# Attention feeding a mixture of experts: where the routing weights are multiplied in, and in which order the first layer's products run

## The chip, the core and the metric

The kernel runs on one core of one Trainium2 chip. That core has five engines with instruction queues of their own, each taken in order: TensorE (PE in the profile: matmuls, with PEld for its weight loads), VectorE (DVE), ScalarE (ACT), GpSimd (POOL) and SyncE (SP, which only issues transfers). They wait for each other through semaphores. The metric is the device time of one execution in microseconds, as the median of several.

## The reference, cut to what matters

The first half is attention over 4 batches, 8 heads, 768 positions and 64 features. Three heads use a full causal mask; five see only 4 first positions and a window of 64. Its result, put back into rows of 512 features, is the input of the second half, in which every token goes through all four experts, weighted by normalised probabilities:

```python
scores = scale * np.matmul(q, k.transpose(0, 1, 3, 2))
scores = np.where(mask[None, :, :, :], scores, -1000000000.0)
a = softmax(scores)                       # cut: written out in the reference
attn_out = np.matmul(a, v)
x = np.ascontiguousarray(attn_out.transpose(0, 2, 1, 3)).reshape(B * S, H * D)   # 3072 x 512

p = domain_probs / (domain_probs.sum(-1, keepdims=True) + 1e-09)
for e in range(E):                        # E = 4 experts, 512 -> 1024 -> 512
    h = np.maximum(x @ w1[e], 0.0)
    out += p[:, e:e + 1] * (h @ w2[e])
```

## The kernel before

Tokens are in 24 tiles of 128. Attention is made in eight groups of 384 positions (three tiles each), numbered 0 to 7. The first four tiles go through the experts in a plain way; the other twenty in ten pairs of tiles (`pair_steps`; here pair 0 to pair 9, tiles 4 and 5 to tiles 22 and 23). Attention of later groups is recorded between the steps of the experts: every step of the experts yields its nominal time and a share, and a plan tells how far each attention group should be once so much weighted time is spent.

Because p is positive, p * relu(x @ w1) is relu((p * x) @ w1). So VectorE multiplies the input of each expert by that expert's probabilities first. This is one instruction of 1024 elements per partition, or two of 512 where a pair straddles two attention groups. The factors, `pB`, are fp32 and come by a transfer into a single buffer.

```python
def scale_inputs(nt0, e):
    ...                                   # cut: xs = scaled(e), the slot of expert e
    for g, c0, t0, n in pieces(nt0):
        require(g)                        # attention group g is recorded to its end first
        ...
        nc.vector.tensor_tensor(          # L1078
            out=o, in0=xin, in1=pb.to_broadcast([P, DMP, n, P]), op=ALU.mult
        )
```

A pair's first layer treats experts 0 and 1 as ordinary products (`plain_layer1`, L1115: eight steps of eight matmuls 128 x 256, each step ended by a ReLU on ScalarE), and experts 3 and 2 (`EW`) by a Winograd scheme with seven half-size products instead of eight. Each product is eight matmuls of 128 columns (L1144). Partial results are kept by ScalarE (`keep`) and added by VectorE (`add`, L1160, followed by a clamp at zero, L1166). Each expert has two banks of PSUM, x and y, which its products share; the second expert takes the same two in reverse, so a product often has to wait until the previous content of its bank has been read:

```python
product(x, w1_part(e, 0, 0), x_part(e, 0, 0), True);  keep(0, x)          # 1
product(z, w1_part(e, 1, 0), x_part(e, 0, 1), True);  add(0, z, 0)        # 2
product(x, t(1), x_sum(1), False);                    keep(1, x)          # 3
product(y, t(0), x_sum(0), True);                     keep(2, y)          # 4
minus(x_part(e, 0, 1), x_part(e, 0, 1), x_sum(1))
product(x, w1_part(e, 0, 1), x_part(e, 1, 0), False); add(2, x, 3)        # 5
product(y, w1_part(e, 1, 1), x_part(e, 0, 1), False); add(1, y, 2)        # 6
product(x, t(2), x_part(e, 1, 1), False)              # 7, then ReLU on ScalarE
# cut: a yield (ns, 0.5) after each product
```

`scaled_sums(e)` makes x_sum(0), x_sum(1) and a difference out of the scaled input (three VectorE instructions; L1092 and L951). The order of the first layer, with a for the products of expert 3, b for those of expert 2 and n01 for plain steps of experts 0 and 1:

```python
for steps, op in (
    ((a, a, n01), lambda: scale_inputs(nt0, EW[1])),
    ((a, a, n01), lambda: scale_inputs(nt0, 1)),
    ((a, n01), lambda: scaled_sums(EW[1])),
    ((a, a, n01), lambda: load_probs(nxt) if nxt is not None else None),
    ((b, b, n01), lambda: first_sum(0)),
    ((b, b, n01), lambda: first_sum(EW[0])),
    ((b, n01), lambda: last_weight_sum(E - 1) if nt0 == pair0 else None),
    ((b, b, n01), None),
):
```

The second layer runs over all four experts at once, also with seven products, of sixteen matmuls with 256 columns each (L1228). In between VectorE makes sums of hidden blocks in place (`second_sum`, `third_sum`, `fourth_sum`, L951), and the two first scalings of the next pair stand near the end:

```python
yield from product(x, A11, b(0, 0), True);  keep(0, x);  second_sum(0); second_sum(1)   # 1
yield from product(y, A12, b(1, 0), True);  add(0, y, 0, 0);  third_sum(0)              # 2
yield from product(x, S2, t(1), False);     keep(1, x);  third_sum(1)                   # 3
yield from product(y, S1, t(0), True);      keep(2, y);  fourth_sum(0); fourth_sum(1)   # 4
yield from product(x, S3, b(0, 1), False);  add(2, x, 1, 1);  scale_inputs(nxt, 0)      # 5
yield from product(y, S4, b(1, 1), False);  add(1, y, 0, 1);  scale_inputs(nxt, EW[0])  # 6
yield from product(x, A22, t(2), False);    scaled_sums(EW[0])                          # 7
# cut: yields, stores of the result, the conditions for the last pair
```

Of the kernel before, what the change touches and what calls it, by code (L numbers as in the profile page):

```python
# [10 lines left out]
FP32 = mybir.dt.float32  # L11
# [7 lines left out]
def kernel(  # L19
# [34 lines left out]
    P = 128  # L54
    B, H, S, D = q.shape
    E, DM, F = moe_w1.shape
# [474 lines left out]
    def mm_ns(cols):  # L531
        return cols / 2.4 + 2.5

    def attention(b, c):
# [282 lines left out]
        if first:  # L817
            yield from transposes(0)
            yield from scores(0)
            sink_row(1)  # L820
            sink_row(3)
            nc.scalar.copy(out=bS[:, 2, :], in_=bS[:, 1, :])
            yield from transposes(1)
            yield from scores(2)
            sink_row(4)
            sink_row(5)
            sink_row(7)
            yield from both(scores(1), values(0))
            yield from transposes(2)
            yield from both(scores(3), values(2))  # L830
            x_transposes(0)
            yield from scores(4)
            yield from transposes(3)
            yield from values(1)
            yield from both(scores(5), values(3))
            yield from both(scores(6), values(4))
            yield from both(scores(7), values(6))
            yield from values(5)
            x_transposes(6)
            yield from values(7)  # L840
            tick(LAG)
            small_things()
        else:
            order = (0, 2, 6, 1, 3, 5, 7, 4) if by_dma else (0, 2, 1, 3, 6, 5, 7, 4)
            more = divmod(g + 1, NCH) if g + 1 < G else None
            if not by_dma:
                sink_rows(b, c)

            def behind_values(h):
                if more and not RETR[h]:  # L850
                    load_v(*more, [h])
            if by_dma:
                keys_to_rows(b, c)
                yield 500.0
            else:
                yield from transposes(0)
                yield from transposes(1)

            waiting = []
            for n, h in enumerate(order):  # L860
                v_steps, done = iter(()), None
                ahead = sum(len(score_tiles(x)) for x in (*waiting, h))
                if len(waiting) > 1 or (waiting and ahead > 6):
                    done = waiting.pop(0)
                    v_steps = values(done)
                yield from both(scores(h), v_steps)
                if done is not None:
                    behind_values(done)
                waiting.append(h)
                if n == 1 and by_dma:  # L870
                    keys_to_windows(b, c)
                    sink_rows(b, c)
                if n == 3 and more and g > 1:
                    transpose_k(*more)

                    load_q(*more)
                if not by_dma and n in (1, 3):
                    yield from transposes({1: 3, 3: 2}[n])
            if more:
                if g == 1:  # L880
                    load_probs(pair0)
                    transpose_k(*more)
                transpose_q(*more)
            for h in waiting:
                yield from values(h)
                behind_values(h)
# [154 lines left out]
    PT = 2  # L1041
# [25 lines left out]
    def scale_inputs(nt0, e):  # L1067

        if xs_of[0] is None:
            xs_of[0] = moe.tile([P, E * DMP * PC], FP16, name="xs", tag="xs", bufs=1)  # L1070
        xs = scaled(e)
        for g, c0, t0, n in pieces(nt0):
            require(g)
            xin = xT[g][:, :, c0 : c0 + n * P].rearrange("p c (t x) -> p c t x", t=n)
            o = xs[:, :, t0 * P : (t0 + n) * P].rearrange("p c (t x) -> p c t x", t=n)
            pb = pB_of[nt0][:, t0 : t0 + n, e, :]
            pb = pb.rearrange("p t (c x) -> p c t x", c=1)
            nc.vector.tensor_tensor(  # L1078
                out=o, in0=xin, in1=pb.to_broadcast([P, DMP, n, P]), op=ALU.mult
            )  # L1080
# [9 lines left out]
    def scaled_sums(e):  # L1090

        nc.vector.tensor_tensor(  # L1092
            out=x_sum(0), in0=x_part(e, 1, 0), in1=x_part(e, 1, 1), op=ALU.add
        )
        minus(x_sum(1), x_sum(0), x_part(e, 0, 0))
        minus(x_part(e, 1, 0), x_part(e, 0, 0), x_part(e, 1, 0))
# [5 lines left out]
        )  # L1102


    PSHARE = 1.57

    def pair_steps(nt0, nxt):

        def plain_layer1(e):
            xs = scaled(e)  # L1110
            for f0 in range(0, FTP, 2):
                ps = bank()
                for f in range(2):
                    for ct in range(DMP):
                        nc.tensor.matmul(  # L1115
                            out=ps[:, f * PC : (f + 1) * PC],
                            lhsT=w1sb[:, e * DMP + ct, (f0 + f) * P : (f0 + f + 1) * P],
                            rhs=xs[:, ct, :],
                            start=(ct == 0),
                            stop=(ct == DMP - 1),  # L1120
                        )
                b0 = 2 * (f0 // HT)
                k0 = e * HT + f0 % HT
                nc.scalar.activation(  # L1124
                    out=blocks[:, b0 : b0 + 2, k0 : k0 + 2, :].rearrange(
                        "p t f x -> p f t x"
                    ),
                    in_=ps.rearrange("p (f t x) -> p f t x", f=2, t=2),
                    func=AF.Relu,
                )  # L1130
                yield 2 * DMP * mm_ns(PC), 0.5

        s1 = moe.tile([P, 4 * HN], FP32, name="s1", tag="sums", bufs=1)
        kept = [s1[:, (n % 2) * HT * P : (n % 2 + 1) * HT * P] for n in range(3)]
# [2 lines left out]
        def winograd_layer1(e, x, y):  # L1137
# [34 lines left out]

            product(x, w1_part(e, 0, 0), x_part(e, 0, 0), True)
            keep(0, x)
            yield ns, 0.5
            z = bank()
            product(z, w1_part(e, 1, 0), x_part(e, 0, 1), True)
            add(0, z, 0)
            yield ns, 0.5
            product(x, t(1), x_sum(1), False)  # L1180
            keep(1, x)
            yield ns, 0.5
            product(y, t(0), x_sum(0), True)
            keep(2, y)
            minus(x_part(e, 0, 1), x_part(e, 0, 1), x_sum(1))
            yield ns, 0.5
            product(x, w1_part(e, 0, 1), x_part(e, 1, 0), False)
            add(2, x, 3)
            yield ns, 0.5
            product(y, w1_part(e, 1, 1), x_part(e, 0, 1), False)  # L1190
            add(1, y, 2)
            yield ns, 0.5
            product(x, t(2), x_part(e, 1, 1), False)
            nc.scalar.activation(
                out=block(1), in_=x.rearrange("p (f x) -> p f x", f=HT), func=AF.Relu
            )
            yield ns, 0.5

        a, b = (winograd_layer1(e, *y) for e, y in zip(EW, (banks, banks[::-1])))
        n01 = itertools.chain(plain_layer1(0), plain_layer1(1))
        for steps, op in (
            ((a, a, n01), lambda: scale_inputs(nt0, EW[1])),
            ((a, a, n01), lambda: scale_inputs(nt0, 1)),
            ((a, n01), lambda: scaled_sums(EW[1])),
            ((a, a, n01), lambda: load_probs(nxt) if nxt is not None else None),
            ((b, b, n01), lambda: first_sum(0)),
            ((b, b, n01), lambda: first_sum(EW[0])),
            ((b, n01), lambda: last_weight_sum(E - 1) if nt0 == pair0 else None),  # L1210
            ((b, b, n01), None),
        ):
            for x in steps:
                yield next(x)
            if op is not None:
                op()
        first_sum(1)
        first_sum(EW[1])

        o = moe.tile([P, PT, DM], FP32, name="o", bufs=1)  # L1220
        s = moe.tile([P, 4 * HN], FP32, name="s", tag="sums", bufs=1)
        s = s.rearrange("p (n x) -> p n x", n=4)
        y = pO.tile([P, DM], FP32, name="pO", bufs=2)[:, 0:HN]
        x = pO.tile([P, DM], FP32, name="pO", bufs=2)[:, 0:HN]

        def product(ps, a, b, first):
            for k in range(KT):
# [41 lines left out]
            minus(S4[:, k, :], A12[:, k, :], S2[:, k, :])  # L1269

        last = nxt is None
        half = KT // 2 * mm_ns(HN), PSHARE
        yield from product(x, A11, b(0, 0), True)
        keep(0, x)
# [3 lines left out]
        yield from product(y, A12, b(1, 0), True)  # L1278
        add(0, y, 0, 0)
        third_sum(0)  # L1280
        yield half
        yield from product(x, S2, t(1), False)
        keep(1, x)
        third_sum(1)
        yield half
        yield from product(y, S1, t(0), True)
        keep(2, y)
# [2 lines left out]
        yield half  # L1290
        yield from product(x, S3, b(0, 1), False)
        add(2, x, 1, 1)
        if nxt is not None:
            scale_inputs(nxt, 0)
        yield half
        yield from product(y, S4, b(1, 1), False)
        add(1, y, 0, 1)
        if nxt is not None:
            scale_inputs(nxt, EW[0])
        store(0)  # L1300
        if last:
            store(1, 1)
# [74 lines left out]

    plan = {1: (1.15 * UNIT, 3.5 * UNIT)}
    begin = E * UNIT + 0.6 * ONE
    for a, n in zip(range(2, G), (0.72, 1.65, 3.2, 4.65, 6.2, 7.65)):  # L1380
        plan[a] = (begin, first_pair + n * PAIR)
        begin = plan[a][1]
    loads(2)
# [77 lines left out]
```

## Time and profile before

| | |
|---|---|
| median of 3 runs | 399.17 us (398.18 to 400.43) |
| span of the profiled run | 396.3 us |
| TensorE busy | 372.4 us |
| VectorE busy | 306.9 us |
| ScalarE busy | 229.6 us |
| granted TensorE clock | 1.0 |
| first pair's first layer begins at | 92.7 us |
| last second layer begins at | 380.7 us |

How to read the views. A row of instructions has the line in the kernel, the engine, the operation, output and inputs by tile name and their shapes, and then a count with busy time or durations. A row of the waits says which engine's instruction stood idle, for what, how many microseconds in all, how often, and the longest. A stage row gives for one stretch (from and to in microseconds) its length and each engine's busy time. Drawn ends of matmuls are modelled: the next one starts before the drawn end of the one in front, so distances from start to start say more than gaps between drawn bars.

### The profile page before, as it was taken

Reading aid. Unit: us, or ns where it says so; the run is one execution under the profiler, and the core shown is the slowest. Engines: PE = TensorE matmul, PEld = TensorE weight load, DVE = VectorE, ACT = ScalarE, POOL = GpSimd, SP = SyncE. Lnnn points to the kernel's source line nnn. Section 1 sums busy time; section 2 is a strip of 40 time slices with the busy share of each in tenths; the row PEclk is TensorE's granted clock in tenths of the full one; section 3 lists DMA queues with packets and bytes.
Section 4 is the critical chain, followed back from the end, with each engine's and each line's share of the span. In section 5 each row is a group of like instructions: output and inputs, shape, how many; then the busy total and the mean of one; then the engine's idle time right before and its main releaser. Section 6 shows DMA issues by size and latency. Waiting matters only on the chain.

```text
span 396.3 us, 10589 instructions
## 1 busy us (share of the span) xinstructions
PE 372.4 (94%) x4294; PEld 312.3 (79%) x4294; DVE 306.9 (77%) x714; ACT 229.6 (58%) x476; POOL 110.4 (28%) x152
## 2 busy tenths in 40 slices
PE   8989999999899898799899999889999999999996
PEld 4755456667798897689788898779988889988895
DVE  7736687799897888977867978977967877866861
ACT  3853559547686775565565675556565665351640
POOL 8833653850335055123500135222100000000000
PEclk9999999999999999999999999999999999999999
DMA  8999999993999799898910499994810210110101
GB/s 161 156 208 199 183 183 177 160 190 57 139 87 128 89 87 99 133 110 78 158 31 14 105 120 87 138 118 38 116 55 13 68 55 2 57 52 0 55 2 53
DMA packets 127197, 39.25 MB, mean 99 GB/s; under 512 B 116232, under 2 KB 120876, under 8 KB 127148
## 3 DMA queue, kind: packets, MB, share of 16 engines
q0 software_dynamic: 86816, 19.01, 54.4%
q1 hardware_dynamic: 38732, 19.18, 21.9%
q8 instruction: 33, 0.54, 0.6%
q10 hardware_dynamic: 1600, 0.39, 0.5%
q14 instruction: 16, 0.13, 0.1%
HBM read 44.88 MB, written 6.34 MB: 129 GB/s over the span
## 4 chain that ended last, share of the span: by engine, by line
PE 56%; DVE 26%; DMA 9%; issue 3%; ACT 3%; POOL 1%; SPq 1%; DVEq 0%; ACTq 0%; POOLq 0%
PE pO L1228 24%; PE pA L1115 10%; PE pO L1144 8%; DVE xs L1078 7%; DMA w2sb<-in_moe_w_dram 7%; DVE hA L1160 4%; PE pA L653 4%; PE pO L1017 3%; PE pA L996 3%; DMA qT<-rows 2%; DVE kS L291 2%; DVE es L675 1%; PE pV L765 1%; PE pV L701 1%; ACT es L671 1%
## 5 line engine op out<-in xcount | busy, mean ns | idle before, releaser
L1228 PEld LDWEIGHTS <-hA 128*128 128x128 f16 x1120 | 106.2, 98 | 12.6
L1115 PE MATMUL pA<-xs,w1sb 128*128 128x256 f16 x640 | 82.9, 273 | 0.0
L671 ACT ACTIVATE es<-pA 128x384 f16<-128x384 f32 (+2 forms) x122 | 59.4, 512 | 36.1 <-PE pA L653 33.5
L1228 PE MATMUL pO<-w2sb,hA 128*128 128x256 f16 x640 | 78.1, 273 | 0.0
L1124 ACT ACTIVATE hA<-pA 128x512 f16<-128x512 f32 x80 | 47.8, 599 | 29.5 <-PE pA L1115 27.3
L1115 PEld LDWEIGHTS <-w1sb 128*128 128x128 f16 x640 | 58.9, 98 | 5.5
L1228 PE MATMUL pO<-tsb,hA 128*128 128x256 f16 x480 | 58.9, 273 | 0.0
L1078 DVE TENSOR_TENSOR xs<-xT,pB 128x1024 f16<-128x1024 f16 (+1 forms) x52 | 49.5, 970 | 0.0
L1144 PEld LDWEIGHTS <-w1sb 128*128 128x128 f16 x640 | 39.6, 98 | 5.9 <-issue 3.4
L307 POOL DMA_DIRECT2D vS<-in_v_dram x30 | 29.0, 970 | 45.3 <-PE pV L765 44.9
L1144 PEld LDWEIGHTS <-t1sb 128*128 128x128 f16 x480 | 29.3, 98 | 13.1 <-issue 10.2
L951 DVE TENSOR_TENSOR hA<-hA 128x1024 f16<-128x1024 f16 x60 | 39.0, 684 | 0.2
L1144 PE MATMUL pO<-xs,w1sb 128*128 128x128 f16 x480 | 36.6, 219 | 2.4 <-DVE hA L1160 1.8
L212 POOL DMA_DIRECT2D rows<-in_q_dram x15 | 13.4, 900 | 86.8 <-DMA kT<-rows 86.8
L1154 ACT COPY s<-pO 128x512 f32<-128x512 f32 x60 | 33.6, 591 | 6.1 <-PE pO L1144 3.7
L1009 ACT ACTIVATE hA<-pA 128x384 f16<-128x384 f32 (+1 forms) x64 | 22.2, 386 | 18.2 <-PE pA L996 17.8
L1160 DVE TENSOR_TENSOR hA<-pO,s 128x512 f16<-128x512 f32 x40 | 27.4, 686 | 6.6 <-PE pO L1144 6.0
L996 PE MATMUL pA<-xT,w1sb 128*128 128x384 f16 (+1 forms) x256 | 31.5, 273 | 0.1
L1017 PE MATMUL pO<-w2sb,hA 128*128 128x512 f16 x128 | 30.5, 379 | 0.7 <-DMA w2sb<-in_moe_w_dram 0.7
L788 DVE TENSOR_TENSOR xT<-pV,rc 64x384 f16<-64x384 f32 x37 | 20.5, 555 | 8.6 <-ACT rc L793 6.2
L783 ACT ACTIVATE rc<-pV,eps 64x384 f32<-64x384 f32 x37 | 21.3, 575 | 9.9 <-PE pV L765 8.9
L996 PEld LDWEIGHTS <-w1sb 128*128 128x128 f16 x256 | 19.2, 98 | 8.2 <-issue 0.5
(134 smaller groups left out, 528.2 us busy)
## 6 DMA issues: line engine op xcount, KB each, us to landing
pB<-p_rows SPq DMA_DIRECT2D x10, 512.0 KB, 3.9
out_dram<-o SPq DMA_DIRECT2D x19, 256.0 KB, 4.9
w1sb<-in_moe_w_dram POOLq DMA_DIRECT2D x8, 512.0 KB, 10.7
w2sb<-in_moe_w_dram POOLq DMA_DIRECT2D x4, 1024.0 KB, 13.5
vS<-in_v_dram POOLq DMA_DIRECT2D x30, 112.0 KB, 3.9
rows<-in_k_dram POOLq DMA_DIRECT2D x18, 128.0 KB, 4.5
rows<-in_q_dram POOLq DMA_DIRECT2D x15, 128.0 KB, 4.9
vR<-in_v_dram POOLq DMA_DIRECT2D x24, 48.0 KB, 4.8
```

The source lines that it names most:

```text
L307: gp.dma_start(out=t[:, :, own_v(h)], in_=windows_of(v, b, h, c))
L671: nc.scalar.activation(out=es[:, 0:cols], in_=ps[:, 0:cols], func=AF.Exp, scale=SC)
L951: nc.vector.tensor_tensor(out=out, in0=a, in1=b, op=ALU.subtract)
L996: nc.tensor.matmul(out=pss[ft][:, 0:cols_n], lhsT=w1sb[:, e * DMP + ct, ft * P : (ft + 1) * P], rhs=x[:, ct, :], start=(n == 0), stop=(n = ...
L1017: nc.tensor.matmul(out=ps_o, lhsT=hs[:, ft, j * P : (j + 1) * P], rhs=w2sb[:, e * FTP + ft, :], start=(ft == 0), stop=(ft == FTP - 1),)
L1078: nc.vector.tensor_tensor(out=o, in0=xin, in1=pb.to_broadcast([P, DMP, n, P]), op=ALU.mult)
L1115: nc.tensor.matmul(out=ps[:, f * PC : (f + 1) * PC], lhsT=w1sb[:, e * DMP + ct, (f0 + f) * P : (f0 + f + 1) * P], rhs=xs[:, ct, :], start= ...
L1124: nc.scalar.activation(out=blocks[:, b0 : b0 + 2, k0 : k0 + 2, :].rearrange("p t f x -> p f t x"), in_=ps.rearrange("p (f t x) -> p f t x" ...
L1144: nc.tensor.matmul(out=ps[:, f * P : (f + 1) * P], lhsT=w[:, ct, f * P : (f + 1) * P], rhs=a[:, ct, :], start=(first and f == 0 and ct == ...
L1154: nc.scalar.copy(out=kept[n], in_=ps)
L1160: nc.vector.tensor_tensor(out=block(b), in0=ps.rearrange("p (f x) -> p f x", f=HT), in1=kept[n].rearrange("p (f x) -> p f x", f=HT), op=AL ...
L1228: nc.tensor.matmul(out=ps, lhsT=a[:, k, :], rhs=b(k), start=(first and k == 0), stop=(k == KT - 1), skip_group_check=not first,)
```

## The change

All scalings of a pair are moved out of its own first layer where the pair is a late one: with `dense` false (pairs 3 to 9) all four scaled inputs are made during the second layer of the pair in front. In pairs 0 to 2 two of the four stay in the first layer, at other places. The first layer's products are put in another order, so that more matmuls stand between a sum on VectorE and the product that needs its bank. The shares that guide attention change from 0.5 to 0.4 in first layers and from 1.57 to 1.65 in second layers, the plan's ends change with them, and the key transposes and query loads of the next group are issued one head earlier. The purpose is to take VectorE work out of the stretches in which TensorE waits for VectorE.

```diff
-                if n == 3 and more and g > 1:
+                if n == 2 and more and g > 1:
                     transpose_k(*more)
                     load_q(*more)
...
-    PSHARE = 1.57
+    LSHARE, PSHARE = 0.4, 1.65
+    def dense(nt0):
+        return nt0 < pair0 + 3 * PT
...
-            yield ns, 0.5
+            yield ns, LSHARE
             # the same for each product and each plain step
...
+        early_on = dense(nt0)
         for steps, op in (
-            ((a, a, n01), lambda: scale_inputs(nt0, EW[1])),
-            ((a, a, n01), lambda: scale_inputs(nt0, 1)),
-            ((a, n01), lambda: scaled_sums(EW[1])),
-            ((a, a, n01), lambda: load_probs(nxt) if nxt is not None else None),
-            ((b, b, n01), lambda: first_sum(0)),
-            ((b, b, n01), lambda: first_sum(EW[0])),
-            ((b, n01), lambda: last_weight_sum(E - 1) if nt0 == pair0 else None),
-            ((b, b, n01), None),
+            ((a, a, n01), lambda: scale_inputs(nt0, EW[1]) if early_on else None),
+            ((a, a, n01), lambda: load_probs(nxt) if nxt and not early_on else None),
+            ((a, a, n01), lambda: scale_inputs(nt0, 1) if early_on else None),
+            ((n01,), lambda: scaled_sums(EW[1])),
+            ((a, b, n01), lambda: first_sum(0)),
+            ((b, b, n01), lambda: load_probs(nxt) if nxt and early_on else None),
+            ((b, b, n01), lambda: last_weight_sum(E - 1) if nt0 == pair0 else None),
+            ((b, n01, b), lambda: first_sum(EW[0])),
         ):
...
+        x = pO.tile([P, DM], FP32, name="pO", bufs=2)[:, 0:HN]
         y = pO.tile([P, DM], FP32, name="pO", bufs=2)[:, 0:HN]
-        x = pO.tile([P, DM], FP32, name="pO", bufs=2)[:, 0:HN]
...
+        ahead = nxt and not dense(nxt)
...
         yield from product(y, A12, b(1, 0), True)
         add(0, y, 0, 0)
         third_sum(0)
+        if ahead:
+            scale_inputs(nxt, 1)
         yield half
         yield from product(x, S2, t(1), False)
         keep(1, x)
         third_sum(1)
+        if ahead:
+            scale_inputs(nxt, 0)
         yield half
...
-        if nxt is not None:
-            scale_inputs(nxt, 0)
+        if nxt:
+            scale_inputs(nxt, EW[0] if ahead else 0)
...
-        if nxt is not None:
-            scale_inputs(nxt, EW[0])
+        if nxt:
+            scale_inputs(nxt, EW[1] if ahead else EW[0])
...
-    for a, n in zip(range(2, G), (0.72, 1.65, 3.2, 4.65, 6.2, 7.65)):
+    for a, n in zip(range(2, G), (0.72, 1.65, 3.1, 4.3, 5.95, 7.38)):
```

More of the change, by code (lines that the diff above doesn't have):

```diff
@@ L1130, in plain_layer1 @@
                 )
-                yield 2 * DMP * mm_ns(PC), 0.5
+                yield 2 * DMP * mm_ns(PC), LSHARE
         s1 = moe.tile([P, 4 * HN], FP32, name="s1", tag="sums", bufs=1)
@@ L1178, in winograd_layer1 @@
             add(0, z, 0)
-            yield ns, 0.5
+            yield ns, LSHARE
             product(x, t(1), x_sum(1), False)
             keep(1, x)
-            yield ns, 0.5
+            yield ns, LSHARE
             product(y, t(0), x_sum(0), True)
@@ L1185, in winograd_layer1 @@
             minus(x_part(e, 0, 1), x_part(e, 0, 1), x_sum(1))
-            yield ns, 0.5
+            yield ns, LSHARE
             product(x, w1_part(e, 0, 1), x_part(e, 1, 0), False)
             add(2, x, 3)
-            yield ns, 0.5
+            yield ns, LSHARE
             product(y, w1_part(e, 1, 1), x_part(e, 0, 1), False)
             add(1, y, 2)
-            yield ns, 0.5
+            yield ns, LSHARE
             product(x, t(2), x_part(e, 1, 1), False)
@@ L1196, in winograd_layer1 @@
             )
-            yield ns, 0.5
+            yield ns, LSHARE
         a, b = (winograd_layer1(e, *y) for e, y in zip(EW, (banks, banks[::-1])))
         n01 = itertools.chain(plain_layer1(0), plain_layer1(1))
+        early_on = dense(nt0)
         for steps, op in (
-            ((a, a, n01), lambda: scale_inputs(nt0, EW[1])),
-            ((a, a, n01), lambda: scale_inputs(nt0, 1)),
-            ((a, n01), lambda: scaled_sums(EW[1])),
-            ((a, a, n01), lambda: load_probs(nxt) if nxt is not None else None),
-            ((b, b, n01), lambda: first_sum(0)),
-            ((b, b, n01), lambda: first_sum(EW[0])),
-            ((b, n01), lambda: last_weight_sum(E - 1) if nt0 == pair0 else None),
-            ((b, b, n01), None),
+            ((a, a, n01), lambda: scale_inputs(nt0, EW[1]) if early_on else None),
[6 more added lines that the diff above has]
+            ((b, n01, b), lambda: first_sum(EW[0])),
         ):
@@ L1214, in pair_steps @@
                 yield next(x)
-            if op is not None:
-                op()
+            op()
         first_sum(1)
```

## The prediction

> **What bounds the kernel now.** I read the page first, then the stage table (busy time of each engine in chosen stretches), TensorE's waits, and two engines' timelines in one stretch. The page names TensorE and puts VectorE next:
>
> ```profile
> PE 372.4 (94%) x4294; PEld 312.3 (79%) x4294; DVE 306.9 (77%) x714; ACT 229.6 (58%) x476; POOL 110.4 (28%) x152
> ```
>
> A 94% engine leaves 396.3 - 372.4 = 23.9 us to win, so the question is where these lie. Cutting the stretch from 92.7 us to the end at the first matmul of each layer gives ten first layers and ten second layers. Four first layers (pairs 0, 2, 5, 8), then four second layers (pairs 3, 4, 5, 7); columns: stretch, length, busy time of PE, PEld, DVE, ACT, POOL, clock, DMA:
>
> ```profile
> 92.70:110.00 17.30, 14.94 (x224) 13.76 (x221) 15.63 (x44) 11.60 (x22) 3.67 (x4) 1.00 0.88 112
> ...
> 158.90:176.20 17.30, 15.00 (x217) 13.47 (x214) 15.48 (x46) 10.27 (x20) 3.50 (x5) 1.00 0.78 117
> ...
> 250.50:268.40 17.90, 14.96 (x218) 13.56 (x216) 15.30 (x47) 10.54 (x20) 2.65 (x3) 1.00 0.77 118
> ...
> 340.80:354.70 13.90, 13.60 (x179) 12.57 (x177) 10.77 (x27) 8.85 (x16) 0.00 (x0) 1.00 0.19 70
> ```
> ```profile
> 205.40:221.80 16.40, 16.40 (x200) 14.52 (x198) 12.51 (x32) 8.93 (x19) 0.00 (x0) 1.00 0.10 24
> 236.60:250.50 13.90, 13.90 (x154) 12.39 (x151) 11.81 (x26) 7.80 (x16) 7.77 (x9) 1.00 1.20 94
> 268.40:281.90 13.50, 13.47 (x161) 12.03 (x157) 10.80 (x20) 7.91 (x16) 4.47 (x5) 1.00 0.71 73
> ...
> 328.20:340.80 12.60, 12.60 (x128) 11.32 (x127) 10.09 (x20) 4.79 (x10) 0.00 (x0) 1.00 0.02 8
> ```
>
> In the heavy first layers VectorE is busier than TensorE (15.63 against 14.94 in pair 0) and TensorE stands; in most second layers TensorE is full and VectorE has about 2 to 4 us free. Over all ten first layers length minus PE busy is 157.4 - 144.6 = 12.9 us. TensorE's waits over the same part say for whom:
>
> ```profile
> PE pO L1144 <- DVE hA L1160: 9.7, 15, 1.5
> PE pO L1144 <- DVE kS L951: 1.0, 1, 1.0
> ```
>
> And the worst one, in pair 5, in VectorE's timeline (start, duration, instruction) and then in TensorE's:
>
> ```profile
> 254.96 1.29 DVE L1078 TENSOR_TENSOR xs<-xT,pB 128x512 f16<-128x512 f16 x2
> ...
> 257.04 1.28 DVE L1078 TENSOR_TENSOR xs<-xT,pB 128x512 f16<-128x512 f16 x2
> 258.24 0.69 DVE L1160 TENSOR_TENSOR hA<-pO,s 128x512 f16<-128x512 f32 x1
> ```
> ```profile
> 256.84 0.61 PE L1144 MATMUL pO<-xs,w1sb 128*128 128x128 f16 x8
> 258.98 0.22 PE L1144 MATMUL pO<-xs,t1sb 128*128 128x128 f16 x1 [1.52 <-DVE hA L1160]
> ```
>
> The last product of expert 3 writes the bank that the add on L1160 must read first; that add stands in VectorE's queue behind two scalings for experts 2 and 1. Of the ten such places I add up the time from the start of the matmul before to the start of this one, less the 56 ns that a 128-column matmul takes in a full row (16 take 0.89 us): 1.36, 1.19, 1.43, 1.40, 0.66, 1.69, 0.27, 0.87, 0.29, 0.15, together 9.3 us. From start to start all first-layer gaps are 17.3 us and second-layer ones 2.5 us; the waits view shows less because a matmul's drawn end runs on.
>
> [...] A scaling has an fp32 factor (pB): [...] The trace has 1216 ns, and 684 ns for a 1024-element subtraction in fp16. So scalings are the dearest VectorE instructions here, and moving them, not shrinking them, is what this change does. [...]
>
> **The change part by part.** The same matmuls, scalings, sums and attention work are issued before and after. With equal arithmetic, time can come only from idle TensorE.
>
> 1. *Order of first-layer products, all ten pairs.* An add and its clamp cost 0.69 + 0.31, near 0.97 us from start to start. Expert 3's steps 5, 6, 7 ran as 5, plain step, 6, 7; now 5, 6, plain, plain, 7. A product is 8 x 56 ns = 0.44 us, a plain step 8 x 109 ns = 0.87 us, so between the end of product 5 and product 7, which waits for its sum, lie 0.44 + 1.74 = 2.2 us instead of 0.87 + 0.44 = 1.3. The first product of expert 2 waits for the sum of product 6 and likewise gets 2.2 instead of 1.3; those places cost 0.83 + 0.12 + 0.34 + 0.34 + 0.16 + 0.16 + 0.34 + 0.43 + 0.34 + 0.34 = 3.4 us before. Expert 2's own last product goes from 1.3 to 2.2 too (0.18 + 0.61 us before).
>
> 2. *Scalings of pairs 3 to 9 moved into the second layer in front.* Two of four move per pair, 2 x 1.2 = 2.4 us of VectorE out of a first layer that holds 10.5 to 15.3 us, into a second layer that holds 8.0 to 12.7 us.
>
> Parts 1 and 2 together in pairs 3 to 9: expert 3's gaps 1.40 + 0.66 + 1.69 + 0.27 + 0.87 + 0.29 + 0.15 = 5.3, expert 2's first 0.34 + 0.16 + 0.16 + 0.34 + 0.43 + 0.34 + 0.34 = 2.1, last 0.6: 8.0 us. With VectorE at about 9 to 12 us in 13.5 us I leave 0.7: gain 7.3 us.
>
> In pairs 0 to 2 the scalings stay, only behind the adds. Gaps there are 1.36 + 1.19 + 1.43 + 0.83 + 0.12 + 0.34 + 0.18 = 5.45 us, but VectorE is itself full (15.6 of 17.3), and the scaling for expert 1 now stands one step ahead of its reader: adds 2 x 0.97, then 1.22, so 3.2 us after product 5 ends, where its reader starts after 0.44 + 1.74 + 0.44 + 0.44 = 3.1 us. Some wait returns. Gain 2.9 us, a bit over half.
>
> 3. *What the second layers pay.* In pair 3 VectorE is 12.5 busy of 16.4; 2.4 more and the larger attention share (part 4) bring it close to 16. The tight spot is the fourth sum, which product 6 reads: in the trace it ends its first half at 216.86 and its reader starts at 217.09, 0.2 us later. Ahead of it VectorE stood idle some 1.0 us (before 209.84), 0.8 (before 211.85) and 0.75 (before 213.43) while waiting, so part of two new scalings (2.4 us) fits there; I take 0.8 us as wait. Pair 4 ends with VectorE already late: its sums let the next pair wait 1.13 us (start to start) now, and 2.4 us more with only 2.1 free (13.9 - 11.8) make it worse. Estimates for what each second layer, with the start of the next pair, loses: pair 2 0.8, pair 3 0.8, pair 4 2.0, pair 5 0.4, pair 6 0.8, pair 7 0.2, pair 8 0.1: 5.1 us.
>
> 4. *Attention's share: 0.5 to 0.4 in first layers, 1.57 to 1.65 in second.* At 13.2 us and 12.2 us per pair the weighted sum goes from 6.6 + 19.2 to 5.3 + 20.1, so the first layers' part falls from 26% to 21%. Counted in the order of instructions, attention matmuls in first layers fall from 1.08 to 0.37 us in pair 5, and rise in pair 3's second layer from 4.1 to 4.6. This is inside the sums above.
>
> 5. *Key transposes and query loads one head earlier.* The next queries land sooner. TensorE waits for them twice (0.24 and 0.93 us start to start); 0.9 us come back.
>
> Sum: 7.3 + 2.9 - 5.1 + 0.9 = 6.0 us. 399.2 - 6.0 = 393.2; I say 393.
>
> **The rivals.**
>
> *VectorE becomes the bound of second layers.* For it: it reaches almost TensorE's length there, and third and fourth sums are in a chain with products 5 and 6. Against it: VectorE's total (306.9 us) is the same and a late scaling has 1.8 us (two products and a plain step) to the reader of the last sums. If it wins, part 3 doubles to 10 us, 7.3 + 2.9 - 10 + 0.9 leaves 1 us, and the time is about 398.
>
> *The gaps were not caused by scalings, but by the order of products.* For it: pairs 8 and 9, without attention, wait in the same places, if only 0.5 to 0.6 us. Then part 1 alone brings perhaps 5 of the 7.3 us, and part 2 only its price: 5 + 2.9 - 5.1 + 0.9 = 3.7, so 395.5.
>
> *Both fit.* If the scheduled idle time of VectorE in second layers (2 to 4 us each) takes the scalings without a wait, the loss of part 3 is 1 to 2 us and the time 389 to 390. For it: the two scalings that stand there already cost TensorE at most 0.2 us within the second layer in pairs 2 to 8.
>
> *An earlier drain of attention.* Scaling pair 5 in pair 4's second layer needs the attention group of its second token tile half a pair earlier. The plan ends that group at 4.3 instead of 4.65 pairs for this. If it comes late, VectorE's queue stands for it: 1 to 2 us.
>
> **Range and chances.** Gains of parts 1 and 2 I trust within 2 us, the loss of part 3 only within 3. Together 389.5 to 397 should hold it 8 times in 10. Faster by over 2% means below 391.2: the third rival or a share of it, 0.32. Slower by over 2% would need over 8 us of new waits beyond the gains, 0.03. Between: 0.65.
>
> **What will show it.** Right: the row of L1160's add in TensorE's waits falls from 9.7 to under 3 us; first layers of pairs 3 to 9 are 13.3 to 14.5 us long, with VectorE at 9 to 11; second layers of pairs 2 to 7 have VectorE within 1 us of their length, and TensorE waits for the sums on L951 or for the scalings, about 5 us in all. Wrong: first layers still 15 us and over in pairs 3 and 5 (then scalings weren't the cause), or second layers longer by over 1.5 us each (then VectorE is the bound), or new waits for DMA.

## The result, and the profile after

The changed kernel takes 394.68 us as the median of 4 runs (393.71 to 396.23), the kernel before in the same comparison 398.83 us. The ratio is 0.9894, with a 95% interval from 0.9848 to 0.9939: 0.6 to 1.5% faster. A second comparison gave 394.15 us and 0.987 (0.9838 to 0.9903). The profiled span fell from 396.3 to 392.0 us. In the code after, lines are shifted: L1148 is the former L1144 (half-size products), L1119 is L1115 (plain steps), L1164 is L1160 (adds), L1233 is L1228 (second layer).

Busy time of each engine, from the page of the changed kernel:

```profile
PE 370.7 (95%) x4294; PEld 312.4 (80%) x4294; DVE 308.0 (79%) x714; ACT 228.1 (58%) x476; POOL 111.8 (29%) x152
```

The same work is there. Stages of the changed kernel, in the columns used before and here in order of time: the first layers of pairs 0 and 2, the second layers of pairs 3 and 4, both layers of pair 5, the second layer of pair 7 and the first of pair 8.

```profile
92.90:110.10 17.20, 14.94 (x223) 13.74 (x220) 15.20 (x42) 11.18 (x22) 3.68 (x4) 1.00 0.71 106
...
161.30:177.70 16.40, 14.45 (x209) 13.27 (x204) 15.01 (x44) 9.80 (x19) 4.35 (x6) 1.00 1.12 133
...
205.10:222.60 17.50, 17.27 (x219) 15.22 (x219) 15.50 (x38) 10.90 (x24) 0.00 (x0) 1.00 0.20 32
...
236.90:253.10 16.20, 15.10 (x171) 13.15 (x169) 15.50 (x42) 6.77 (x16) 5.88 (x7) 1.00 0.71 56
253.10:267.40 14.30, 13.74 (x194) 12.75 (x191) 11.02 (x31) 10.37 (x20) 3.64 (x4) 1.00 0.94 140
267.40:280.60 13.20, 13.20 (x152) 11.89 (x150) 12.15 (x21) 6.88 (x14) 3.85 (x4) 1.00 0.72 66
...
325.20:337.60 12.40, 12.40 (x123) 11.13 (x121) 11.69 (x22) 3.34 (x8) 0.00 (x0) 1.00 0.02 8
337.60:350.90 13.30, 13.30 (x179) 12.57 (x178) 8.27 (x23) 8.40 (x16) 0.00 (x0) 1.00 0.19 74
```

Read the rows in pairs with those of before. Pair 5's first layer went from 17.90 to 14.30 us, with VectorE at 11.02 instead of 15.30. Pair 8's is TensorE from end to end. In pair 0 hardly anything has changed: 17.20 us instead of 17.30, VectorE at 15.20 instead of 15.63. The second layers of pairs 3 and 4 are longer by 1.1 and 2.3 us; about 0.5 us of each is attention that moved there with the shares.

TensorE's waits in the changed kernel, from the first pair on:

```profile
PE pO L1148 <- DVE xs L951: 3.3, 3, 1.6
PE pA L653 <- DMA qT<-rows: 2.0, 1, 2.0
PE pO L1148 <- DVE kS L951: 1.9, 2, 1.3
PE pA L653 <- DVE kR L275: 1.2, 1, 1.2
PE pA L1119 <- DVE xs L1078: 0.9, 2, 0.5
PE pA L653 <- DVE kS L295: 0.8, 1, 0.8
```

The row of 9.7 us for the adds is gone. In its place stand waits for a difference (L951 on xs), for the queries' transposes, for the sums (L951 on kS) and for key copies. Gaps counted from start to start, as in the prediction, say where the time moved (us). In pairs 3 to 9 the wait of product 3 for its sums is put to the second layer in front, as the prediction did; in pair 2 (1.0 us before, 1.5 after) it stands with the first layers. A wait at the border of two layers can be put to either, so the split between rows is good to some 0.3 us:

| | before | after | gain | predicted |
|---|---|---|---|---|
| first layers, pairs 3 to 9 | 8.0 | 0.9 | 7.1 | 7.3 |
| first layers, pairs 0 to 2 | 7.2 | 6.9 | 0.3 | 2.9 |
| second layers of pairs 2 to 8 | 2.5 | 3.6 | -1.1 | -5.1 |
| second layers of pairs 0 and 1 | 2.1 | 3.9 | -1.8 | 0.9 |
| sum | 19.8 | 15.3 | 4.5 | 6.0 |

The span fell by 4.3 us and the time by 4.2.

### The profile page after: what moved, and what is told of

It is laid out like the page before. It is cut to its first block, busy times and chain, and to the rows that moved or that the text cites. A ratio compares the mean times of both kernels' runs of the same rounds, so it can differ in the third digit from the quotient of the medians.

```text
span 392.0 us, 10589 instructions
## 1 busy us (share of the span) xinstructions
PE 370.7 (95%) x4294; PEld 312.4 (80%) x4294; DVE 308.0 (79%) x714; ACT 228.1 (58%) x476; POOL 111.8 (29%) x152
## 4 chain that ended last, share of the span: by engine, by line
PE 65%; DVE 16%; DMA 8%; ACT 4%; POOL 3%; issue 3%; SPq 0%; DVEq 0%; POOLq 0%; ACTq 0%
PE pO L1233 26%; PE pA L1119 13%; PE pO L1148 10%; DMA w2sb<-in_moe_w_dram 7%; PE pA L653 4%; DVE xs L1078 3%; PE pO L1017 3%; PE pA L996 3%; DVE hA L1164 2%; PE pA L1148 2%; DVE kS L291 2%; DMA qT<-rows 2%; PE pV L765 2%; PE pV L701 1%; ACT es L671 1%
## 5 line engine op out<-in xcount | busy, mean ns | idle before, releaser
L1233 PEld LDWEIGHTS <-hA 128*128 128x128 f16 x1120 | 105.8, 98 | 12.9 <-issue 0.5
L1119 PE MATMUL pA<-xs,w1sb 128*128 128x256 f16 x640 | 82.0, 273 | 0.9 <-DVE xs L1078 0.9
L1233 PE MATMUL pO<-w2sb,hA 128*128 128x256 f16 x640 | 77.8, 272 | 0.3 <-DVE hA L1164 0.2
L1119 PEld LDWEIGHTS <-w1sb 128*128 128x128 f16 x640 | 59.2, 98 | 7.0 <-DVE xs L1078 1.3
L1233 PE MATMUL pO<-tsb,hA 128*128 128x256 f16 x480 | 59.3, 272 | 0.1
L1148 PEld LDWEIGHTS <-w1sb 128*128 128x128 f16 x640 | 39.6, 98 | 5.4 <-DVE xs L951 3.7
L951 DVE TENSOR_TENSOR hA<-hA 128x1024 f16<-128x1024 f16 x60 | 39.5, 684 | 0.6 <-PE pO L1233 0.5
L1148 PE MATMUL pO<-xs,w1sb 128*128 128x128 f16 x480 | 35.6, 219 | 3.4 <-DVE xs L951 3.3
L1164 DVE TENSOR_TENSOR hA<-pO,s 128x512 f16<-128x512 f32 x40 | 27.5, 688 | 13.5 <-ACT s L1158 8.0
L1158 ACT COPY s<-pO 128x512 f32<-128x512 f32 x60 | 34.6, 589 | 5.6 <-PE pO L1148 4.0
L1148 PEld LDWEIGHTS <-t1sb 128*128 128x128 f16 x480 | 30.2, 98 | 3.7 <-DVE kS L951 2.6
L653 PE MATMUL pA<-qT,kR 128*128 128x384 f16 (+2 forms) x120 | 22.6, 278 | 5.1 <-DVE kR L275 2.4
```

Of the source, the lines that this page charges most:

```text
L653: nc.tensor.matmul(out=ps[:, o : o + nq], lhsT=key_tile(b, c, h, t), rhs=qTs[b, c][:, hp, q0 : q0 + nq], start=(n == 0 or not first), stop ...
L951: nc.vector.tensor_tensor(out=out, in0=a, in1=b, op=ALU.subtract)
L1119: nc.tensor.matmul(out=ps[:, f * PC : (f + 1) * PC], lhsT=w1sb[:, e * DMP + ct, (f0 + f) * P : (f0 + f + 1) * P], rhs=xs[:, ct, :], start= ...
L1148: nc.tensor.matmul(out=ps[:, f * P : (f + 1) * P], lhsT=w[:, ct, f * P : (f + 1) * P], rhs=a[:, ct, :], start=(first and f == 0 and ct == ...
L1158: nc.scalar.copy(out=kept[n], in_=ps)
L1164: nc.vector.tensor_tensor(out=block(b), in0=ps.rearrange("p (f x) -> p f x", f=HT), in1=kept[n].rearrange("p (f x) -> p f x", f=HT), op=AL ...
```

## The experiments

The theory: scalings in VectorE's queue and the order of products together made the first-layer gaps; second layers had room for what moved there. Rivals: the order alone; the shares and the plan; earlier loads. Unless said otherwise each kernel is the changed one with one thing altered, and is compared with its 394.15 to 394.68 us.

### The former order (old_order)

```diff
-    ((n01,), lambda: scaled_sums(EW[1])),
-    ((a, b, n01), lambda: first_sum(0)),
+    ((a, n01), lambda: scaled_sums(EW[1])),
+    # and so on: steps as before the change, scalings as after it
```

> The changed kernel with the first layer's products (and the two banks of the second layer) in their former order; scalings stay moved. If the scalings in VectorE's queue made the first-layer gaps: pairs 3 to 9 keep at most 1.5 us of gaps in first layers (10.1 before the change, 1.9 after) and the time is 0.5 to 2 us above the changed kernel's 394.7. If the order of products made them: 5 us or more of gaps come back there and the time is near 399.

Measured: 397.46 us, ratio to the kernel before 0.9951 (0.993 to 0.9971). First layers of pairs 3 to 9 have 3.3 us of gaps by start-to-start counting (1.9 after the change, 10.1 before, product 3's waits included). The waits in the stretch of pairs 3 to 9 are for the adds again, but small:

```profile
PE pO L1148 <- DVE hA L1164: 1.2, 4, 0.6
```

The gaps are between the two expectations, the nearer one being the first (1.5 us at most). The time lost 2.8 us, which is more than the first expectation. In pairs 0 to 2 the waits of the first layers add up to some 7.2 us, much as after the change (6.9). Twice in this trace, in pair 0 and in the second layer of pair 1, the granted clock was 0.50 for 3.41 us. So I don't assign more than the 1.4 us of late pairs to the order; where the rest of the 2.8 us lies is open.

### No scaling moved (no_move)

```diff
     def dense(nt0):
-        return nt0 < pair0 + 3 * PT
+        return True
```

> The changed kernel with all pairs treated as early ones: new order, no scaling moved. If the order alone closes the gaps: first layers of pairs 3 to 9 have under 3 us of gaps, second layers lose their new waits, time 393 to 395. If the scalings have to go: gaps of 1 us and more stay in each first layer with attention (as in pairs 0 to 2 after the change, 1.8 to 2.8 us each), 6 to 9 us in all, and the time is 397 to 400.

Measured: 397.34 us, ratio 0.9946 (0.9923 to 0.9968). The gaps in first layers of pairs 3 to 9 are 5.8 us, and their releaser is now a scaling itself, in the waits from pair 3 on:

```profile
PE pA L1119 <- DVE xs L1078: 1.9, 4, 0.8
PE pO L1148 <- DVE xs L951: 1.1, 2, 0.9
PE pO L1148 <- DVE xs L1078: 0.7, 2, 0.5
```

With the order new, the adds no longer hold up product 7, but the scaling for expert 1 holds up the plain step that reads it. The gaps are a little under the second expectation's 6 to 9 us, the time is inside its range. So neither alone: undoing the order costs 2.8 us, undoing the moves 2.7 us, and the gaps say that the moves are the larger part (5.8 against 3.3 us left, of 10.1 before and 1.9 after). The clock doesn't make these losses: the executions at a granted clock of 1.000 alone have medians of 396.4 us (old_order, nine) and 396.5 us (no_move, eight), against 393.7 and 394.1 us for two of the changed kernel.

### The former shares and plan (old_shares)

```diff
-    LSHARE, PSHARE = 0.4, 1.65
+    LSHARE, PSHARE = 0.5, 1.57
-    (0.72, 1.65, 3.1, 4.3, 5.95, 7.38)
+    (0.72, 1.65, 3.2, 4.65, 6.2, 7.65)
```

> The changed kernel with the former shares (0.5 and 1.57) and plan. If the larger attention share in second layers makes the two new waits of attention in pairs 0 and 1 (1.40 and 2.20 us from start to start after, 0.24 and 0.93 before): they fall to about 1.2 together, and against that a wait of 1 to 2 us for group 5 in pair 4; time 393 to 395. If the shares are what the change lives on: 397 or more.

Measured: 394.56 us, ratio 0.9879 (0.9838 to 0.9919), no difference to the changed kernel. In pair 0 the wait of 1.40 us for keys is gone and one of 0.56 us for queries stands at its place, but the query wait in pair 1 stayed at 2.08, so the two are 2.6 us together, not 1.2. The wait that was expected in pair 4 came, 1.26 us for keys, and product 6 of the second layer now waits 0.37 us in pair 3 and 0.92 in pair 7. So the shares only move waits about: they are neither what the change lives on nor, alone, the cause of the query wait.

### Key transposes and query loads one head later (late_loads)

```diff
-                if n == 2 and more and g > 1:
+                if n == 3 and more and g > 1:
```

> The changed kernel with key transposes and query loads one head later, as before. If the earlier loads bring the 0.9 us of my part 5: 395.5 to 396.5. If they cause the new wait for the queries in pair 1 (2.2 us): it is gone and the time is 392.5 to 393.5. If neither: within 0.5 us of 394.7.

Measured: 393.79 us, ratio 0.9848 (0.9802 to 0.9894). The interval reaches the changed kernel's ratios, 0.987 and 0.9894, and the time is 0.4 to 0.9 us below its times; none of the three expectations fits well. In this trace the query wait in pair 1 is 3.5 us, not less than 2.2, so the earlier loads don't cause it. They hardly come earlier either: counted from the start of pair 1, the first query transpose is issued at 21.86 us in the changed kernel and at 21.85 here, and the query rows are loaded only 0.2 us sooner. With the transposes issued alike, the waits are 2.2, 2.6 (when measured again) and 3.5 us: a wait of this kind seems to vary by 1 us or so from run to run.

### The scaling for expert 2 one step later in pairs 0 to 2 (scale_later)

```diff
-    ((a, a, n01), lambda: scale_inputs(nt0, EW[1]) if early_on else None),
-    ((a, a, n01), lambda: load_probs(nxt) if nxt and not early_on else None),
+    ((a, a, n01), lambda: None),
+    ((a, a, n01), lambda: scale_inputs(nt0, EW[1]) if early_on else load_probs(nxt) ...),
```

> The changed kernel, but in pairs 0 to 2 the scaling for expert 2 is recorded one step later, behind the difference that product 6 reads. If the scaling ahead of that difference makes the waits of 1.72, 1.22 and 0.83 us at product 6: they fall below 0.5 us each, the sum of first-layer gaps in pairs 0 to 2 from 6.9 to 4 to 5 us, the time 2 us lower than the changed kernel. If VectorE is simply full there: the waits move on to product 7 and to the plain step that reads the scaling for expert 1, the sum stays over 6 us, the time within 0.7 us.

This aims at the largest wait that stayed. In pair 0 of the changed kernel, VectorE's timeline, then TensorE's:

```profile
97.41 1.22 DVE L1078 TENSOR_TENSOR xs<-xT,pB 128x1024 f16<-128x1024 f16 x1
98.54 0.28 DVE L951 TENSOR_TENSOR xs<-xs,kS 128x256 f16<-128x256 f16 x1
```
```profile
96.72 0.61 PE L1148 MATMUL pO<-xs,w1sb 128*128 128x128 f16 x8
98.89 0.29 PE L1148 MATMUL pO<-xs,w1sb 128*128 128x128 f16 x2 [1.56 <-DVE xs L951]
```

Product 6 reads the difference x_part(0, 1) - x_sum(1), which stands behind a scaling. Before the change a plain step stood between products 5 and 6; the new order took it away from there.

Measured: 395.98 us, ratio 0.9906 (0.9873 to 0.9938). Of the waits at product 6 only 0.59 us is left, in pair 0, and they have moved on. In the stretch of pairs 0 to 2:

```profile
PE pA L1119 <- DVE xs L1078: 2.8, 3, 1.5
```

The sum of first-layer gaps in pairs 0 to 2 is 7.1 us against 6.9. The second expectation holds for the gaps: this rearrangement only passes the wait on. The time is not better but 1.3 to 1.8 us longer, outside its 0.7 us. The extra goes with the granted clock: the one execution at 1.000 took 394.1 us, the four at 0.991 took 395.8 to 397.4.

### Two scalings left out in pairs 1 and 2 (early_skip)

```diff
-    scale_inputs(nt0, EW[1]) if early_on else None
-    scale_inputs(nt0, 1) if early_on else None
+    scale_inputs(nt0, EW[1]) if nt0 == pair0 else None
+    scale_inputs(nt0, 1) if nt0 == pair0 else None
```

This kernel leaves out those two scalings and uses old values there.

> The changed kernel with the two scalings that stand in the first layers of pairs 1 and 2 left out (old values are used there; all else stays). If VectorE's scalings are what keeps the first layers of pairs 0 to 2 from gaining: the waits at product 6 (1.22 and 0.83 us) and at the plain step (0.54) go, pair 1's first layer has under 0.4 us of gaps, pair 2's only the wait for the sums at its third product (0.7 to 1.5), the time 2 to 3.5 us lower. If attention's VectorE work alone fills them: over half of the gaps stay.

Measured: 392.04 us, ratio 0.9821 (0.979 to 0.9852), 2.1 to 2.6 us below the changed kernel, as the first expectation has it. First-layer waits from pair 1 to the end of pair 2's first layer, in the changed kernel and then here:

```profile
PE pO L1148 <- DVE xs L951: 1.7, 2, 1.1
PE pO L1148 <- DVE kS L951: 1.3, 1, 1.3
PE pA L1119 <- DVE xs L1078: 0.4, 1, 0.4
```
```profile
PE pO L1148 <- DVE kS L951: 0.5, 1, 0.5
```

From start to start, pair 1's first layer has 0.1 us of gaps (1.8 after the change), pair 2's 0.7 (2.4), the latter all for the sums at product 3. So it is the 2.4 us of scalings in these first layers that keeps them from gaining. To move them too, attention's groups would have to end earlier; that wasn't tried.

### The moved scalings done twice (twice)

```diff
         if ahead:
             scale_inputs(nxt, 1)
+            scale_inputs(nxt, 1)
         # and the same for scale_inputs(nxt, 0)
```

> The changed kernel with the two additional scalings in the second layers done twice each (same values again), 2.4 us more of VectorE in each of seven second layers, 17 us in all. If VectorE still has room in second layers (light pairs 5, 7, 8: 1 to 2 us each; heavy ones less): 5 to 9 us slower. If second layers are already bound by VectorE: 12 us or more. If much room was left: under 4 us.

Measured: 413.64 us, ratio 1.0362 (1.0324 to 1.0399), 19 us over the changed kernel for 17 us of VectorE. All of it is in second layers. Some 15 us are waits, from start to start; most of the rest is that the granted clock was 0.50 for 3.41 us in the second layers of pairs 2, 4 and 7, each time when a wait of over 2 us ended. Most of the waiting is at one place, in the waits over the whole run:

```profile
PE pO L1233 <- DVE hA L951: 10.4, 7, 2.3
PE pV L701 <- DVE es L675: 3.4, 2, 2.1
```

The second expectation holds: after the change hardly any room is left. It isn't VectorE's total that is full, though. Pair 8 has no attention, and TensorE waits there too. Pair 8's second layer of the doubled kernel as a stage, with VectorE busy for 12.96 of 14.40 us, then VectorE's timeline and TensorE's:

```profile
368.40:382.80 14.40, 12.47 (x117) 10.88 (x115) 12.96 (x19) 2.00 (x5) 0.00 (x0) 1.00 0.03 9
```

```profile
376.13 2.48 DVE L1078 TENSOR_TENSOR xs<-xT,pB 128x1024 f16<-128x1024 f16 x2
378.53 1.29 DVE L951 TENSOR_TENSOR hA<-hA 128x1024 f16<-128x1024 f16 x2
```
```profile
375.43 1.91 PE L1233 MATMUL pO<-w2sb,hA 128*128 128x256 f16 x16
379.27 0.94 PE L1233 MATMUL pO<-w2sb,hA 128*128 128x256 f16 x7 [1.93 <-DVE hA L951]
```

And the same place in the changed kernel's pair 8, VectorE alone:

```profile
357.31 1.22 DVE L1078 TENSOR_TENSOR xs<-xT,pB 128x1024 f16<-128x1024 f16 x1
358.44 1.28 DVE L951 TENSOR_TENSOR hA<-hA 128x1024 f16<-128x1024 f16 x2
```

Its product 6 is due at 350.88 + 5 x 16 x 109 ns = 359.6 us (in TensorE's timeline there, 32 matmuls take from 357.87 to 361.36 us, start to start, 109 ns each), and the first half of the fourth sum ends near 359.1: 0.5 us of margin. Two more scalings ahead of it are 2.4 us, and the wait is 2.1 us from start to start. What counts is the margin of the fourth sum at product 6; in pairs 3 and 4 it is that of attention's masks (the row on L701, which waits for es), behind the same scalings.

### Window loads left out (no_v3 and no_v4)

Both leave out five loads of V windows for one attention group (its five heads with the short window, the streaming ones, then use old values); all else stays.

```diff
-                if more and not RETR[h]:
+                if more and not RETR[h] and g != 2:      # no_v3; g != 3 in no_v4
```

> The changed kernel without the five window loads of V for attention group 3 (its streaming heads then use old values: this load is left out, all other work stays). If these loads crowd the DMA engines and so delay the query transposes that pair 1 waits for: the wait of 2.2 us in pair 1 falls under 0.5 us and the time by 1.5 to 2.5 us. If the transposes were issued too late by themselves: the wait stays over 1.5 us.

Measured: 394.84 us, ratio 0.9886 (0.9846 to 0.9925); query wait in pair 1: 3.3 us. This run was aimed wrong: the loads for group 3 are made in pair 0, those in flight when pair 1 waits are for group 4. It says nothing for or against.

> The changed kernel without the five window loads of V for attention group 4, which are the ones under way while pair 1 waits for group 4's queries (the run before left out group 3's, which are loaded in pair 0). Left out is this load alone. If these loads crowd the DMA engines: the wait for the query transposes in pair 1 (2.2 us, 2.6 when measured again) falls under 0.7 us, the time by 2 to 3 us. If not: the wait stays over 1.5 us.

Measured: 391.98 us, ratio 0.9815 (0.9782 to 0.9848), 2.2 to 2.7 us below the changed kernel. The query wait is all but gone (0.35 us from start to start). Its row in the kernel before, and here:

```profile
PE pA L653 <- DMA qT<-rows: 0.8, 1, 0.8
```
```profile
PE pA L653 <- DMA qT<-rows: 0.2, 1, 0.2
```

The three query transposes are issued at the same places in both kernels, 4.83, 6.12 and 7.43 us after the first product of pair 1's second layer; the second of them landed 5.2 us after its issue in the changed kernel and 2.4 us after it here. So the query transposes, issued by SyncE, are slowed by window loads issued by GpSimd at the same time, here by 2.8 us. In what way the loads hold them up was not measured.

### Key copies ahead of the scalings (early_keys and early_keys_all)

```diff
                 transpose_q(*more)
+                if g > 1:
+                    keys_to_rows(*more)
+                    keys_to_windows(*more)    # in early_keys_all alone
```

The copies at their former place fall away for these groups.

> The changed kernel with the copies of the next group's retrieval keys recorded right after its query transposes, and so ahead of the scalings in VectorE's queue. The wait of 1.40 us for them in pair 0 goes; if nothing takes its place the time is 1 to 1.5 us lower than the changed kernel's (394.2 to 394.7). If the queries are only just there anyway: under 0.5 us.

Measured: 393.63 us in 6 runs, ratio 0.9863 (0.9831 to 0.9895). The wait of 1.40 us for keys in pair 0 is gone, and a wait of 0.8 us for queries stands in its place. The time is 0.5 to 1.0 us below the changed kernel's, between the two expectations; the interval overlaps the changed kernel's, so this is no proven improvement.

> As the one before, with the window copies of the next group's keys (about 2 us of VectorE) recorded there too. The wait of 0.97 us for them in pair 4 and part of the wait for the sums at the third product in pairs 2 and 5 (1.46 and 0.72 us) go: 2 to 3 us lower than the changed kernel. If VectorE's 2 us at that place hold up the third and fourth sums of the second layer: no gain, or slower by up to 2 us.

Measured: 394.30 us, ratio 0.9877 (0.9846 to 0.9909), no gain. The 2 us of window copies hold up the sums of the second layer, three times and up to 1.5 us:

```profile
PE pO L1238 <- DVE hA L956: 4.3, 3, 1.5
```

### The changed kernel again (after_again)

> The changed kernel again, for comparison on the same chip: 394.7 within 1 us, a ratio of 0.985 to 0.994 to the kernel before.

Measured: 394.15 us, ratio 0.987 (0.9838 to 0.9903), as expected.

## Why the prediction was right, and where its parts were not

The time, 394.7 us, lies in the range (389.5 to 397) and 1.7 us above the predicted 393; the gain was 4.2 us instead of 6.2. Four parts stand behind the sum.

- **Parts 1 and 2 in pairs 3 to 9: right in mechanism and size.** Predicted 7.3 us, measured 7.1. With product 3's waits, 10.1 us of gaps stood there before: the order alone leaves 5.8 us of them, the moves alone 3.3, both together 1.9. The moves do more, and the two overlap. The rival that the order alone made the gaps is refuted by no_move, though the order alone closes nearly half of them.
- **Part 1 in pairs 0 to 2: wrong.** Predicted 2.9 us, measured 0.3. The adds' waits did go, but as much came in elsewhere. The step that failed is the list of waiters: I counted slack for product 7, for expert 2's first product and for the plain step that reads the scaling for expert 1, and overlooked product 6, which reads a difference that VectorE makes behind the scaling for expert 2. "Only behind the adds" holds for the scaling for expert 1 alone; the one for expert 2 stands in these pairs where it stood, behind product 2 and ahead of that difference. The slack of product 6 shrank by the plain step that the new order moves away. Waits of 1.72, 1.22 and 0.83 us were there after the change; the trace before had one already, 0.67 us in pair 0, which the prediction's sum left out. Moving that scaling passes the wait on (scale_later), leaving the scalings out removes it (early_skip).
- **Part 3: right in kind, too large.** Predicted 5.1 us, measured 1.1, which is what the rival "Both fit" had for it (1 to 2 us). The mis-sized term is 0.8 us at product 6 for heavy pairs and 2.0 us for pair 4: no second layer of the changed kernel waits at product 6. In pair 3 the idle stretches that the prediction lists, 1.0 + 0.8 + 0.75 us, are as long as the two new scalings (2.4 us), and I credited them with only a part. Pair 3 paid some 0.5 us more in its second layer, none of it at product 6; pair 4 paid 1.6, of which 0.97 is for key windows, and the next pair's wait for its sums even fell from 1.13 to 0.72 us. The rival that VectorE becomes the bound was wrong for the change as made, but by little: the same 2.4 us once more made every one of the seven second layers 2 to 4 us longer (half clock included).
- **Part 5: wrong in sign.** Predicted 0.9 us back; measured 1.8 us lost in pairs 0 and 1. The step that failed is "the next queries land sooner": in pair 1 their transposes are issued at the same place with the loads early or late (21.86 and 21.85 us after the pair's start), and later than before the change (20.4 us). The wait in pair 0 is for key copies that stand behind a scaling in VectorE's queue. The wait for queries in pair 1 was 2.2 us, and the window loads in flight beside the query transposes make it (0.35 us without them, no_v4). Undoing the order, the moves, the shares or the earlier loads, each alone, leaves it at 2.1 to 3.5 us. Why it is more than before the change is open: in the kernel before, the two kinds of transfer overlap too, with a wait of 0.93 us in its one profile. In old_shares, which waits 2.08 us, the transposes and the window loads are issued at the same places in that second layer as before the change, to within 0.02 us, so their places there don't explain it; part of it may be the spread from run to run.

The errors are +4.0 in part 3, -2.6 in pairs 0 to 2, -2.7 in part 5 and -0.2 in the rest, together -1.5 us: the total was near because they cancel, and that is luck. The sign that I gave first, the adds' row below 3 us, came true: that row is gone. So did one sign of being wrong, a new wait for DMA: the row for the queries' transposes went from 0.8 to 2.0 us.

The fourth rival, an early drain of attention in pair 4, did not show as a wait for attention's results. Pair 4's second layer did lose 1.6 us, at attention's own key windows and masks.

## What to carry to other kernels

When an in-order engine's work is moved from a stage where it is short of time into one where it isn't, size the price by the margin of the one consumer behind it there (0.5 us at product 6 in pair 8), not by the stage's busy shares: 2.4 us in each of seven stages cost 1.1 us of waits in all, the next 2.4 some 15. When matmuls are reordered to give one consumer more slack, list every consumer between the old and the new place, for the filler that helps one may be taken from another. A transfer's latency is part of the path too: look at what else is in flight when it is issued (here five window loads, without which the query wait fell from 2.2 to 0.35 us).

## What the runs showed of the hardware

A TensorE that waited sometimes lost more than the wait. In the second profile of the changed kernel the query wait was 2.6 us (start to start), and the clock granted behind it fell to half. Stages around it, with the clock in the third column from the end, ahead of DMA share and GB/s:

```profile
154.00:156.00 2.00, 0.59 (x6) 0.39 (x4) 1.94 (x6) 0.00 (x0) 0.00 (x0) 1.00 2.26 114
156.00:158.00 2.00, 0.97 (x5) 0.67 (x5) 0.36 (x1) 0.35 (x1) 0.46 (x1) 0.69 0.09 5
158.00:160.00 2.00, 2.00 (x12) 1.35 (x10) 0.93 (x4) 0.53 (x3) 2.00 (x3) 0.50 0.62 40
160.00:162.00 2.00, 2.00 (x19) 1.71 (x18) 1.81 (x5) 1.44 (x3) 2.00 (x4) 0.95 1.62 109
```

That second layer took 19.4 us, against 17.5 in the first profile, with a wait of 2.2 us and a clock of 1.00; the next first layer got 0.8 us of it back. From the first pair on, up to the last second layer, the profiles here have eight such stretches at 0.50. Each lasted 3.41 us and began within 0.6 us of the matmul that ended a wait: waits of 1.54 and 2.32 us in old_order, 2.13, 2.22 and 2.45 us in twice, 2.60 us here, 2.83 us in early_skip and 3.33 us in no_v3. Other waits as long left the clock at 1.00, among them 2.68 us in early_keys and 3.54 us in late_loads. So a wait of 1.54 us was enough once, and one of 3.54 us was not; what decides between the two was not shown.
